# The last token group's routing: other PSUM banks, another place in the written order, later early gathers

## The chip, the cores and the metric

One core of one Trainium2 chip. The time is the device time of one execution in microseconds (us), the median of several runs; lower is better.

## The reference

Three layers, one after the other, over 3072 tokens (4 sequences of 768) of 384 features.

```python
# 1. delta-rule attention: per sequence and head (8 heads of 48), token after token
y[t] = q[t] @ state
state = state + beta[t] * outer(k[t], v[t] - k[t] @ state)      # k normalised
# 2. one MLP for all tokens: 384 -> 2048 -> 384
h = x @ w_in
x = maximum(0.01 * h, h) @ w_out
# 3. eight experts, each token goes to at most one: 384 -> 1024 -> 384
do = (x @ w_skip) > 0                       # the others are copied to the output
e = argmax(x @ w_gate); gate = softmax(x @ w_gate)[e]
out = x + gate * (maximum(x @ w1[e], 0) @ w2[e])    # where do, else x
```

Below, "the first layer" is layer 2 (`moe1` in the code) and "the experts" are layer 3 (`moe2`).

## The kernel before

Every fp32 operand is split into a high and a low fp16 half, and a product is three matmuls (high x high, high x low, low x high).

**Groups.** Tokens are worked on in 12 groups of 256 (two tiles of 128). A group goes through the attention stages and then the first layer in eight steps of two slices of 128 of the 2048 hidden features. Step `s` is an up (`m_up`, 18 matmuls into a bank `ph`; then ACT, DVE, ACT and POOL make the halves `ghh` and `gll`) and a down (`m_down`, 12 matmuls into two banks `o`). `w_gate` and `w_skip` are folded into ten more columns of `w_out` (columns HD to XW, 384 to 393), so that a down also yields the ten scores of a token. A normal group takes all 394 columns at once and is then routed (`m_fin`, `route`).

**The last group** (`moe1_last`, i = 11) is done apart. Its ups use the pool `h2`. Its downs go twice over the same operands: first only the ten score columns (key "r"), then the 384 others. Both sums are in the pool `ops`, which has two banks: the wide downs get them when ACT has copied the scores to `sc` (L987). Then a thread `last_route` is put at the head of the list of threads.

**Routing** (`route`). DVE and ACT find the best expert as a one-hot row `oh` (L740). After a yield PE counts, with a triangle of ones, the tokens of each expert before this one (`pr`, L746 to L750), DVE turns that into a place `pi` in the expert's part of a list in DRAM (L756 to L761), and POOL scatters the token numbers there, one indirect DMA for each tile of 128 (`lst`, L763). Each of the two waits for the one before. `pr` is in the pool `hps` (one bank, which the first layer's ups used) but for the last group, where it is in `tps` (one bank).

**Tables.** `early` runs after group 10 is routed: it counts (`counts`, a matmul and a copy, L1018 to L1020), finds up to three blocks of 256 tokens of one expert that are full already, and writes their table. `tables`, after the last group's route, counts again and writes the tables of the other blocks. The weights of a block are loaded when its table is there.

**Blocks.** The experts run as 15 blocks: 3 early, 6 big (two tiles of 128), 3 small (128 tokens) and 3 tiny (64). `Block.tokens` reads the block's stretch of the list on SP (`ix`, L1162), gathers its rows from `x2s` with an indirect DMA on POOL for each tile (`xg`, L1165), waits, then transposes them on PE into `pt` in the pool `tps` (L1173), from which ACT and DVE make the halves `xh` and `xl`. `up` and `down` (L1188, L1206 to L1208) follow, then the output is scattered (L1219). Weights come in eight loads of 384 KB for a block (L1138, L1141) through five buffers `ws`, and ACT and DVE split them (L441, L442). `early` calls `tokens` of blocks 0 and 1, the thread `tokens` of those from 2 on, once the tables are written. The rows of the last group are stored to `x2s` by SP (`store`, L714) after its wide downs.

**What sets the order.** Work is written as threads (Python generators). `emit` takes the first thread in its list whose time has come. A `yield a, w` adds `a` to a counter (about microseconds of PE work) and holds the thread for `w` more. What is written earlier has the higher priority, and `high_priority(n)` raises what is in it by n instructions. Dependences follow the written order: an instruction that reads a DRAM tile waits for the earlier written writes to it, and a write for the earlier written reads. A planner then fixes the order of each engine's instructions by priority and by its own estimate of when operands are there; on the chip every engine works off that order. Loads and stores are issued by SP, and its queue is in order too.

Of the kernel before, what the change touches and what calls it, by code (L numbers as in the profile page):

```python
# [8 lines left out]
F32 = mybir.dt.float32  # L9
# [10 lines left out]
HD = H * D  # L20
# [3 lines left out]
NS1 = NF1 // 2  # L24
# [5 lines left out]
XW = HD + 10  # L30
# [463 lines left out]
def tile_kernel(ctx, tc, kq, ktok, vtok, bet, w_in, w_out, w_skip, w_gate, w1, w2, out):  # L494
# [223 lines left out]
    def route(i, sc, t0s, then=lambda: None):  # L718

        L = sc[:, :, 1:9]  # L720
        sk = sc[:, :, 9:10]
        t = lambda nm, shape, dt=F32: rp.tile(shape, dt, tag=nm, name=nm)
        bc = lambda x: x.to_broadcast([128, 2, NE])
        mx, e1, sm, eq, m8, do, oh, ps = (t("mx", [128, 2, 1]), t("e1", [128, 2, NE]), t("sm", [128, 2, 1]),
                                          t("eq", [128, 2, NE]), t("m8", [128, 2, 1]), t("do", [128, 2, 1]),
                                          t("oh", [128, 2, NE], F16), t("ps", [128, 2, NE]))
        nc.vector.tensor_reduce(out=mx, in_=L, axis=AX.X, op=ALU.max)
        nc.vector.tensor_tensor(out=e1, in0=L, in1=bc(mx), op=ALU.subtract)
        nc.scalar.activation(out=e1, in_=e1, func=AF.Exp)
        nc.vector.tensor_reduce(out=sm, in_=e1, axis=AX.X, op=ALU.add)  # L730
        nc.vector.tensor_scalar_add(out=sm, in0=sm, scalar1=1e-9)
        nc.vector.reciprocal(out=sm, in_=sm)
        nc.vector.tensor_scalar_mul(out=sc[:, :, 0:1], in0=sm, scalar1=2.0 ** -13)
        then()
        nc.vector.tensor_tensor(out=eq, in0=L, in1=bc(mx), op=ALU.is_equal)
        nc.vector.tensor_tensor(out=eq, in0=eq, in1=wdesc.unsqueeze(1).to_broadcast([128, 2, NE]), op=ALU.mult)
        nc.vector.tensor_reduce(out=m8, in_=eq, axis=AX.X, op=ALU.max)
        nc.vector.tensor_tensor(out=eq, in0=eq, in1=bc(m8), op=ALU.is_equal)
        nc.vector.tensor_scalar(out=do, in0=sk, scalar1=0.0, scalar2=None, op0=ALU.is_gt)
        nc.vector.tensor_tensor(out=oh, in0=eq, in1=bc(do), op=ALU.mult)  # L740
        yield 0, T["rt"]
        pr = (hps if i < n - 1 else tps).tile([128, 512], F32, tag="h" if i < n - 1 else "t", name="pr")
        acc = acc_state[0]
        prv = pr[:, 0:2 * NE].rearrange("p (j e) -> p j e", j=2)
        for j in range(2):
            nc.tensor.matmul(prv[:, j], lhsT=tri16, rhs=oh[:, j], start=True, stop=(i == 0 and j == 0))  # L746
            if j == 1:
                nc.tensor.matmul(prv[:, j], lhsT=ones16, rhs=oh[:, 0], start=False, stop=(i == 0))
            if i:
                nc.tensor.matmul(prv[:, j], lhsT=ones16, rhs=acc, start=False, stop=True)  # L750
        nacc = t("acc", [128, NE], F16)
        nc.vector.tensor_tensor(out=nacc, in0=oh[:, 0], in1=oh[:, 1], op=ALU.add)
        if i:
            nc.vector.tensor_tensor(out=nacc, in0=nacc, in1=acc, op=ALU.add)
        acc_state[0] = nacc
        nc.vector.tensor_tensor(out=ps, in0=prv, in1=ebase.unsqueeze(1).to_broadcast([128, 2, NE]), op=ALU.add)  # L756
        nc.vector.tensor_tensor(out=ps, in0=ps, in1=oh, op=ALU.mult)
        pf = t("pf", [128, 2, 1])
        nc.vector.tensor_reduce(out=pf, in_=ps, axis=AX.X, op=ALU.add)
        pi = t("pi", [128, 2, 1], I32)  # L760
        nc.vector.tensor_scalar_add(out=pi, in0=pf, scalar1=float(BIG))  # L761
        for j in range(2):
            nc.gpsimd.indirect_dma_start(out=lst[:, :], out_offset=bass.IndirectOffsetOnAxis(ap=pi[:, j, 0:1], axis=0),  # L763
                                         in_=ids[:, t0s[j] // 128:t0s[j] // 128 + 1], in_offset=None,
                                         bounds_check=NL - 1, oob_is_err=False)
# [21 lines left out]
            nc.gpsimd.tensor_tensor(out=gl, in0=g, in1=gh, op=ALU.subtract)  # L787
        ms[i, s] = (gh, gl)

    def m_down(i, s, cols, key):  # L790
        if s == 0:
            ms[key] = [ops.tile([128, XW], F32, tag="o", name="o") for j in range(2)]
        gh, gl = ms[i, s]
        for j in range(2):
            f = 2 * s + j
            for t in range(2):
                ts = slice(t * 128, (t + 1) * 128)
                o = ms[key][t][:, cols]
                nc.tensor.matmul(o, lhsT=gh[:, j, ts], rhs=wo[0][:, f, cols], start=(f == 0), stop=False)  # L799
                nc.tensor.matmul(o, lhsT=gh[:, j, ts], rhs=wo[1][:, f, cols], start=False, stop=False)  # L800
                nc.tensor.matmul(o, lhsT=gl[:, j, ts], rhs=wo[0][:, f, cols], start=False, stop=(f == NF1 - 1))  # L801
            yield (cols.stop - cols.start) / 394, 0
# [175 lines left out]

    def moe1_last():
        i = n - 1  # L980
        for s in range(NS1):
            yield from m_up(i, s, m8 if s < NS1 - LOOK - 2 else m3, h2)
        for s in range(NS1):
            yield from m_down(i, s, slice(HD, XW), "r")
        sc = rp.tile([128, 2, 10], F32, tag="sc", name="sc")
        for t in range(2):
            nc.scalar.activation(out=sc[:, t], in_=ms["r"][t][:, HD:XW], func=AF.Copy, scale=2.0 ** -14)  # L987
        threads.insert(0, Thread(last_route(i, sc), lambda: "early" in state))
        for s in range(NS1):
            yield from m_down(i, s, slice(0, HD), i)  # L990
        xs = m_out(i, i, slice(0, HD))
        nc.vector.tensor_copy(out=xs[:, :, HD:HD + 1], in_=sc[:, :, 0:1])
        store(xs, first(i))
        lctx.close()
        et.append(pool(ctx, "eu", 1, **late))
# [18 lines left out]
    col = lambda x, n: x.unsqueeze(2).to_broadcast([1, x.shape[1], n])  # L1014

    def counts(nm):
        pr = tps.tile([128, 512], F32, tag="t", name="cnt")
        nc.tensor.matmul(pr[:, 0:NE], lhsT=ones16, rhs=acc_state[0], start=True, stop=True)  # L1018
        cnt = t1("cnt" + nm, [NE])
        nc.vector.tensor_copy(out=cnt, in_=pr[0:1, 0:NE])  # L1020
        return cnt
# [40 lines left out]
    def early():  # L1062

        nb = above(counts("e"), 255.5, "e")
        cb = upto(nb, "e")
        a, b, zero, taken = (t1(x, [NE]) for x in ("mine", "mina", "zero", "taken"))
        nc.vector.memset(zero, 0.0)
        table(nb, cb, zero, NEB, "early")
        tt(a, cb, nb, ALU.subtract)
        nc.vector.tensor_scalar_min(out=a, in0=a, scalar1=float(NEB))  # L1070
        nc.vector.tensor_scalar_min(out=b, in0=cb, scalar1=float(NEB))
        tt(taken, b, a, ALU.subtract)
        state["taken"] = taken
        yield 0, 4
        for b in blocks[:NEB - 1]:
            yield from b.tokens()

# [32 lines left out]
    class Block:  # L1110
# [47 lines left out]
        def tokens(self):  # L1158
            nt, R, N = self.nt, self.rows, self.nt * self.rows
            sl = bass.ds(self.entry(1, NL - N), N)  # L1160
            ix = self.idx = e3.tile([128, nt], I32, tag=f"ix{nt}", name="ix")[0:R]
            nc.sync.dma_start(out=ix, in_=lst[sl, :].rearrange("(p j) o -> p (j o)", j=nt))  # L1162
            xg = self.xg = self.tile([128, nt, HD + 1], F32, "xg")[0:R]
            for j in range(nt):
                nc.gpsimd.indirect_dma_start(out=xg[:, j], out_offset=None, in_=x2s[:, :],  # L1165
                                             in_offset=bass.IndirectOffsetOnAxis(ap=ix[:, j:j + 1], axis=0),
                                             bounds_check=NT, oob_is_err=False)
            yield 0, 7
            self.x = xh, xl = [self.tile([128, KD, nt * 128], F16, f"x{x}")[:, :, 0:N] for x in "hl"]
            for j in range(nt):  # L1170
                pt = tps.tile([128, KD, 128], F32, tag="t", name="pt")[:, :, 0:R]
                for d in range(KD):
                    nc.tensor.transpose(pt[:, d], xg[:, j, d * 128:(d + 1) * 128], ident[0:R, 0:R])  # L1173
                ts = slice(j * R, (j + 1) * R)
                nc.scalar.activation(out=xh[:, :, ts], in_=pt, func=AF.Copy, scale=32.0)
                nc.vector.scalar_tensor_tensor(out=xl[:, :, ts], in0=pt, scalar=32.0, in1=xh[:, :, ts], op0=ALU.mult, op1=ALU.subtract)
                yield .4, 1
            self.tok = True
# [106 lines left out]
    te = Thread(early())  # L1285
    tl1 = Thread(moe1_last())
    threads = [te] + threads + [tl1]
    emit(threads, lambda: tl1.done)
    mctx.close()
    threads += [Thread(tokens(), lambda: "nbi" in state), Thread(moe2())]  # L1290
    emit(threads)
# [60 lines left out]
```

## Time and profile before

| | |
|---|---|
| three runs | 1123.02, 1125.24 and 1130.80 us; median 1125.24 us |
| the profiled execution | 1127.62 us, its span 1125.8 us, mean granted TensorE clock 0.906 |
| busy in that span | PE 881.0 us (78%), DVE 724.2 (64%), ACT 658.6 (58%), POOL 500.9 (44%) |
| DMA queue of SP and ACT loads | q1: 123.24 MB, 42.4% of 16 engines' span |

All times in the rows are counted from the start of the span. PE is TensorE's matmul row, PEld its weight loads, SPq the instructions by which SP issues DMAs. A matmul's duration overlaps the next one's, so that the spacing of starts, not the duration, tells what it costs. What stands behind "<-" in a wait is the one that ended it.

### The profile page before, as it was taken

What the parts mean: (1) busy time and instruction counts of PE and PEld (TensorE: products, weight loads), DVE (VectorE), ACT (ScalarE), POOL (GpSimd) and SP (SyncE); (2) the same over time, 40 slices, a digit from 0 to 9 for tenths busy, and PEclk for the clock granted to TensorE, in tenths of its full rate; (3) what the DMA queues carried; (4) which work ended last, traced back from release to release, by engine and by line L of the source; (5) the groups of instructions that cost most, each with busy time, mean ns of one, the idle gap of its engine ahead of it and who ended that gap; (6) DMA issues with size and microseconds to landing.
All of it is one profiled execution on the core that took longest, in us unless ns stands there. A gap on an engine that the chain in (4) does not pass through costs nothing. (4 is left out here: it accounts for less than half of the span.)

```text
span 1125.8 us, 26420 instructions
## 1 busy us (share of the span) xinstructions
PE 881.0 (78%) x10212; PEld 679.8 (60%) x10212; DVE 724.2 (64%) x1599; ACT 658.6 (58%) x1494; POOL 500.9 (44%) x517
## 2 busy tenths in 40 slices
PE   2155887589798868876789797999985948998995
PEld 1144775466676656655667575777763636776763
DVE  5988986586665878655657374434236737887761
ACT  4477686567767767665767465553334516665640
POOL 3556565663365465746464353352243113342111
PEclk9998886589799988978899898999997969999998
DMA  7843876642434456625333322120007638988740
GB/s 207 217 123 101 236 209 177 131 125 37 140 84 95 135 95 196 96 68 121 79 82 64 32 55 39 44 30 29 29 29 178 215 100 251 293 292 279 245 145 17
DMA packets 200865, 144.03 MB, mean 128 GB/s; under 512 B 114318, under 2 KB 183140, under 8 KB 200730
## 3 DMA queue, kind: packets, MB, share of 16 engines
q1 hardware_dynamic: 188416, 123.24, 42.4%
q10 hardware_dynamic: 8570, 10.76, 3.4%
q0 software_dynamic: 3744, 8.27, 2.2%
q8 instruction: 82, 1.34, 0.6%
q14 instruction: 53, 0.43, 0.2%
HBM read 111.91 MB, written 30.92 MB: 127 GB/s over the span
## 5 line engine op out<-in xcount | busy, mean ns | idle before, releaser
L787 POOL TENSOR_TENSOR gll<-gg,ghh 128x512 f16<-128x512 f32 x96 | 114.4, 1194 | 133.7 <-ACT ghh L785 125.3
L783 DVE SCALAR_TENSOR_TENSOR gg<-gg 128x512 f32<-128x512 f32 x96 | 83.2, 868 | 97.6 <-ACT gg L782 97.2
L799 PE MATMUL o<-woh,ghh 128*128 128x394 f16 (+2 forms) x416 | 133.7, 329 | 12.6 <-ACT ghh L785 6.2
L777 PEld LDWEIGHTS <-wih 128*128 128x128 f16 x1152 | 115.7, 103 | 34.2 <-issue 11.9
L801 PE MATMUL o<-woh,gll 128*128 128x394 f16 (+2 forms) x416 | 125.1, 326 | 13.1 <-POOL gll L787 13.0
L800 PE MATMUL o<-wol,ghh 128*128 128x394 f16 (+2 forms) x416 | 133.9, 328 | 0.0
L263 POOL TENSOR_TENSOR gl<-g,gh 128x512 f16<-128x512 f32 x88 | 107.5, 1226 | 45.3 <-ACT gh L262 42.0
L254 ACT ACTIVATE g<-g,d 128x128 f32<-128x128 f32 x384 | 111.4, 384 | 26.7 <-PE g L251 22.4
L777 PE MATMUL ph<-xh,wih 128*128 128x256 f16 x576 | 103.2, 288 | 8.2 <-ACT gg L782 4.1
L255 POOL TENSOR_SCALAR_AFFINE_SELECT g<-g 128x512 f32<-128x512 f32 x96 | 69.3, 722 | 82.7 <-ACT g L254 75.4
L777 PE MATMUL ph<-xh,wil 128*128 128x256 f16 x576 | 102.7, 283 | 0.0
L777 PE MATMUL ph<-xl,wih 128*128 128x256 f16 x576 | 101.4, 286 | 1.1 <-DVE xl L707 1.1
L785 ACT CAST ghh<-gg 128x512 f16<-128x512 f32 x96 | 60.3, 628 | 71.4 <-DVE gg L783 70.5
L782 ACT COPY gg<-ph 128x512 f32<-128x512 f32 x96 | 57.0, 595 | 50.0 <-PE ph L777 46.4
L262 ACT CAST gh<-g 128x512 f16<-128x512 f32 x88 | 55.4, 633 | 35.7 <-POOL g L255 35.3
L442 DVE SCALAR_TENSOR_TENSOR w1l<-ws,w1h 128x768 f16<-128x768 f32 x60 | 57.4, 965 | 26.2 <-ACT w1h L441 24.6
L284 DVE TENSOR_TENSOR tmp<-bt,z 128x15 f32<-128x15 f16 (+4 forms) x180 | 58.7, 326 | 22.2 <-DMA bt<-ai 18.8
L1219 POOL DMA_INDIRECT out_dram<-y,ix x24 | 27.3, 1139 | 102.2 <-DVE y L1217 84.7
L441 ACT ACTIVATE w1h<-ws 128x768 f16<-128x768 f32 x60 | 49.7, 840 | 36.8 <-DMA ws<-in_moe_w_dram 30.4
L1188 PEld LDWEIGHTS <-w1h 128*128 128x128 f16 x720 | 59.1, 100 | 17.3 <-issue 5.5
L1165 POOL DMA_INDIRECT xg<-x2s,ix x24 | 35.6, 1484 | 68.6 <-DMA ix<-lst 48.6
L1206 PE MATMUL o<-w2h,gh 128*128 128x384 f16 (+1 forms) x192 | 63.4, 330 | 1.3 <-ACT gh L1192 1.3
(271 smaller groups left out, 2619.7 us busy)
## 6 DMA issues: line engine op xcount, KB each, us to landing
ws<-in_moe_w_dram SPq DMA_DIRECT2D x120, 384.0 KB
kt<-in_ktok_dram SPq DMA_DIRECT2D x24, 384.0 KB
x<-in_kq_dram SPq DMA_DIRECT2D x22, 384.0 KB
sc<-hl SPq DMA_DIRECT2D x22, 384.0 KB
raw<-in_moe_w_out_dram ACTq DMA_DIRECT2D x16, 384.0 KB
ai<-gh SPq DMA_DIRECT2D x24, 256.0 KB
x2s<-xs SPq DMA_DIRECT2D x24, 192.5 KB
vs<-in_vtok_dram SPq DMA_DIRECT2D x24, 192.0 KB
```

Source lines behind the costliest of these rows:

```text
L254: nc.scalar.activation(out=g32[:, j], in_=g[:, j], func=AF.Copy, scale=k["dd"][:, x, h:h + 1])
L255: nc.gpsimd.affine_select(out=g32, in_=g32, pattern=[[0, 4], [1, C]], compare_op=ALU.is_gt, fill=0.0, base=0, channel_multiplier=-1)
L263: nc.gpsimd.tensor_tensor(out=gl[:, hs], in0=g32, in1=gh[:, hs], op=ALU.subtract)
L777: nc.tensor.matmul(ph[:, j], lhsT=wt[:, d, fs], rhs=xx[:, d], start=(n == 0), stop=(n == 3 * KD - 1))
L783: nc.vector.scalar_tensor_tensor(out=g, in0=g, scalar=0.01, in1=g, op0=ALU.mult, op1=ALU.max)
L785: nc.scalar.copy(out=gh, in_=g)
L787: nc.gpsimd.tensor_tensor(out=gl, in0=g, in1=gh, op=ALU.subtract)
L799: nc.tensor.matmul(o, lhsT=gh[:, j, ts], rhs=wo[0][:, f, cols], start=(f == 0), stop=False)
L800: nc.tensor.matmul(o, lhsT=gh[:, j, ts], rhs=wo[1][:, f, cols], start=False, stop=False)
L801: nc.tensor.matmul(o, lhsT=gl[:, j, ts], rhs=wo[0][:, f, cols], start=False, stop=(f == NF1 - 1))
L1188: nc.tensor.matmul(ph[:, j], lhsT=wt[:, d, fs], rhs=xx[:, d], start=(n == 0), stop=(n == 3 * KD - 1))
L1206: nc.tensor.matmul(o, lhsT=gh[:, j, ts], rhs=wh[:, f], start=(f == 0), stop=False)
```

## The change

Six edits. The last group's `pr` and both `counts` move from `tps` to `hps`. `m_down` takes the pool of its sums, and the last group's scores go to `ops2`, a pool of two banks that the experts use later. The scores of step s - 2 are written after the up of step s, the wide down of step 0 ahead of the last two scores. `last_route` is written with a priority raised by 150. In `early` the list reads and gathers of blocks 0 and 1 are written 12 units behind their table instead of 4. In `tokens` the transposes of every block are written 11 units behind its gathers instead of 7. The first loop of `emit` goes on until the tables are written as well.

```diff
@@ -739,7 +739,7 @@
         nc.vector.tensor_scalar(out=do, in0=sk, scalar1=0.0, scalar2=None, op0=ALU.is_gt)
         nc.vector.tensor_tensor(out=oh, in0=eq, in1=bc(do), op=ALU.mult)
         yield 0, T["rt"]
-        pr = (hps if i < n - 1 else tps).tile([128, 512], F32, tag="h" if i < n - 1 else "t", name="pr")
+        pr = hps.tile([128, 512], F32, tag="h", name="pr")
         acc = acc_state[0]
         prv = pr[:, 0:2 * NE].rearrange("p (j e) -> p j e", j=2)
         for j in range(2):
@@ -787,9 +787,9 @@
             nc.gpsimd.tensor_tensor(out=gl, in0=g, in1=gh, op=ALU.subtract)
         ms[i, s] = (gh, gl)
 
-    def m_down(i, s, cols, key):
+    def m_down(i, s, cols, key, pl=ops):
         if s == 0:
-            ms[key] = [ops.tile([128, XW], F32, tag="o", name="o") for j in range(2)]
+            ms[key] = [pl.tile([128, XW], F32, tag="o", name="o") for j in range(2)]
         gh, gl = ms[i, s]
         for j in range(2):
             f = 2 * s + j
@@ -978,15 +978,19 @@
 
     def moe1_last():
         i = n - 1
+        scores = lambda s: m_down(i, s, slice(HD, XW), "r", ops2)
         for s in range(NS1):
             yield from m_up(i, s, m8 if s < NS1 - LOOK - 2 else m3, h2)
-        for s in range(NS1):
-            yield from m_down(i, s, slice(HD, XW), "r")
+            if s >= LOOK:
+                yield from scores(s - LOOK)
+        yield from m_down(i, 0, slice(0, HD), i)
+        for s in range(NS1 - LOOK, NS1):
+            yield from scores(s)
         sc = rp.tile([128, 2, 10], F32, tag="sc", name="sc")
         for t in range(2):
             nc.scalar.activation(out=sc[:, t], in_=ms["r"][t][:, HD:XW], func=AF.Copy, scale=2.0 ** -14)
-        threads.insert(0, Thread(last_route(i, sc), lambda: "early" in state))
-        for s in range(NS1):
+        threads.insert(0, Thread(high(last_route(i, sc), 150), lambda: "early" in state))
+        for s in range(1, NS1):
             yield from m_down(i, s, slice(0, HD), i)
         xs = m_out(i, i, slice(0, HD))
         nc.vector.tensor_copy(out=xs[:, :, HD:HD + 1], in_=sc[:, :, 0:1])
@@ -1014,7 +1018,7 @@
     col = lambda x, n: x.unsqueeze(2).to_broadcast([1, x.shape[1], n])
 
     def counts(nm):
-        pr = tps.tile([128, 512], F32, tag="t", name="cnt")
+        pr = hps.tile([128, 512], F32, tag="h", name="cnt")
         nc.tensor.matmul(pr[:, 0:NE], lhsT=ones16, rhs=acc_state[0], start=True, stop=True)
         cnt = t1("cnt" + nm, [NE])
         nc.vector.tensor_copy(out=cnt, in_=pr[0:1, 0:NE])
@@ -1071,7 +1075,7 @@
         nc.vector.tensor_scalar_min(out=b, in0=cb, scalar1=float(NEB))
         tt(taken, b, a, ALU.subtract)
         state["taken"] = taken
-        yield 0, 4
+        yield 0, 12
         for b in blocks[:NEB - 1]:
             yield from b.tokens()
 
@@ -1165,7 +1169,7 @@
                 nc.gpsimd.indirect_dma_start(out=xg[:, j], out_offset=None, in_=x2s[:, :],
                                              in_offset=bass.IndirectOffsetOnAxis(ap=ix[:, j:j + 1], axis=0),
                                              bounds_check=NT, oob_is_err=False)
-            yield 0, 7
+            yield 0, 11
             self.x = xh, xl = [self.tile([128, KD, nt * 128], F16, f"x{x}")[:, :, 0:N] for x in "hl"]
             for j in range(nt):
                 pt = tps.tile([128, KD, 128], F32, tag="t", name="pt")[:, :, 0:R]
@@ -1285,7 +1289,7 @@
     te = Thread(early())
     tl1 = Thread(moe1_last())
     threads = [te] + threads + [tl1]
-    emit(threads, lambda: tl1.done)
+    emit(threads, lambda: tl1.done and "nbi" in state)
     mctx.close()
     threads += [Thread(tokens(), lambda: "nbi" in state), Thread(moe2())]
     emit(threads)
```

## Rows read from the trace of the kernel before

**Rows 1.** Busy time by stretches: length, each engine's busy us (instructions), TensorE clock, DMA share, GB/s.
```profile
849.00:862.40 13.40, 1.79 (x45) 1.38 (x42) 4.75 (x10) 4.52 (x9) 4.68 (x4) 0.67 0.86 160
862.40:881.00 18.60, 18.60 (x102) 10.78 (x102) 14.85 (x31) 12.02 (x18) 5.28 (x4) 0.87 0.90 287
...
905.40:920.40 15.00, 0.33 (x4) 0.05 (x2) 1.28 (x8) 0.00 (x0) 3.08 (x3) 0.60 0.52 157
920.40:926.00 5.60, 5.60 (x24) 3.59 (x25) 2.62 (x15) 2.55 (x4) 1.00 (x1) 0.56 0.20 75
926.00:1112.60 186.60, 174.56 (x1530) 126.93 (x1527) 133.95 (x207) 103.97 (x166) 52.18 (x39) 0.98 0.72 229
...
890.00:912.00 22.00, 15.71 (x127) 11.74 (x125) 14.01 (x50) 4.78 (x8) 2.02 (x2) 0.92 0.15 38
```

**Rows 2.** Waits of PE, 849 to 863: who waited for whom, total us, times, longest.
```profile
PE o L799 <- ACT sc L987: 4.3, 1, 4.3
```

**Rows 3.** Timeline of PE, 881 to 921: start us, us, instruction, idle before and releaser.
```profile
884.86 0.52 PE L1173 MATMUL pt<-ident,xg 128*128 128x128 f32 x3 [2.10 <-DMA xg<-x2s,ix]
...
894.41 0.17 PE L746 MATMUL pr<-oh,tri 128*128 128x8 f16 x1
...
904.35 0.33 PE L1207 MATMUL o<-w2l,gh 128*128 128x384 f16 x1
904.51 0.33 PE L1208 MATMUL o<-w2h,gl 128*128 128x384 f16 x1
...
905.00 0.49 PE L1188 MATMUL ph<-xl,w1h 128*128 128x256 f16 x3
905.33 0.38 PE L1188 MATMUL ph<-xh,w1l 128*128 128x256 f16 x2
920.38 0.90 PE L1173 MATMUL pt<-ident,xg 128*128 128x128 f32 x3 [14.68 <-DMA xg<-x2s,ix]
```

**Rows 4.** Lines 1188 and 1206, 881 to 905.5: count, shortest, median, longest ns, starts.
```profile
L1188 PE MATMUL ph<-xl,w1h x39: 270/273/273, 881.7 to 905.2; 128*128 128x256 f16 x39
...
L1206 PE MATMUL o<-w2h,gh x16: 326/326/336, 888.3 to 904.2; 128*128 128x384 f16 x16
```

**Rows 5.** Timeline of ACT around the last group's scores.
```profile
861.44 0.84 ACT L441 ACTIVATE w1h<-ws 128x768 f16<-128x768 f32 x1 [4.55 <-DMA ws<-in_moe_w_dram]
862.19 0.23 ACT L987 ACTIVATE sc<-o 128x10 f32<-128x10 f32 x2
```

**Rows 6.** Timeline of DVE: routing of group 10 and of the last group.
```profile
838.73 0.17 DVE L727 TENSOR_REDUCE mx<-xs 128x2 f32<-128x16 f32 x1 [1.20 <-ACT xs L811]
...
840.60 0.17 DVE L740 TENSOR_TENSOR oh<-eq,do 128x16 f16<-128x16 f32 x1
...
867.86 0.15 DVE L740 TENSOR_TENSOR oh<-eq,do 128x16 f16<-128x16 f32 x1
...
896.12 0.17 DVE L761 TENSOR_SCALAR pi<-pf 128x2 int32<-128x2 f32 x1
```

**Rows 7.** Timeline of POOL: the last group's list scatters and block 2's gather.
```profile
896.57 1.02 POOL L763 DMA_INDIRECT lst<-ids_i,pi  x1 [15.12 <-DVE pi L761]
903.71 1.00 POOL L763 DMA_INDIRECT lst<-ids_i,pi  x1 [6.12 <-DMA lst<-ids_i,pi]
913.59 1.05 POOL L1165 DMA_INDIRECT xg<-x2s,ix  x1 [8.88 <-DMA ix<-lst]
```

**Rows 8.** Timeline of SP's DMA queue.
```profile
910.01 0.34 SPq L1162 DMA_DIRECT2D ix<-lst  x1
```

**Rows 9.** Waits of SP's DMA queue, 881 to 921.
```profile
SPq L1162 <- DMA lst<-ids_i,pi: 19.2, 1, 19.2
SPq L714 <- DMA xg<-x2s,ix: 3.3, 1, 3.3
```

**Rows 10.** Line 763, the 24 list scatters of the whole run.
```profile
DMA to landing us min/median/max: 6.8/7.2/8.8
```

**Rows 11.** Waits of PE, 926 to 1114.
```profile
PE pt L1173 <- DMA xg<-x2s,ix: 8.7, 6, 2.7
```

## The prediction

> **What bounds the kernel now.** I read the 40 slices of the page first, then busy time by stretches around the hand-over from the first layer to the experts, then the waits, last each engine's timeline there. Three things are to be seen.
>
> PE is the busiest engine, but not evenly. From 849 to 862.4 us it works 1.79 of 13.40 us, from 905.4 to 920.4 us 0.33 of 15.00, while in the long stretch from 926 to 1112.6 it is at work for 174.56 of 186.60 us [rows 1]. After 926 nearly every microsecond is PE work, so what is saved before it should reach the end, as long as nothing else takes over. What follows 1112.6 (the last scatters and the ending) isn't touched.
>
> The first hole has several waits in it, the largest for `sc`: 4.3 us [rows 2], since the same two banks hold the narrow score sums and the wide down sums. The second is one wait of 14.68 us: PE stands at the transposes of block 2 until its rows have been gathered [rows 3]. It isn't out of work there. From 881 to 905.4 us 116 up matmuls (39, 39 and 38 of three kinds; one kind is shown) and 48 down matmuls (three kinds of 16) ran [rows 4]; a block of 256 tokens has 72 and 48. So 28 up and 48 down matmuls of block 1 stand behind the transposes in PE's fixed order. By the spacing of starts an up matmul costs 0.33/3 = 0.109 us and a down matmul 0.16 [rows 3]: 28 x 0.109 + 48 x 0.1625 = 10.9 us left of block 1 at 920.4. A whole block is 72 x 0.109 + 48 x 0.1625 + six transposes at 0.11 = 16.3 us.
>
> Why is block 2 late? The last group's choice of experts is ready on DVE at 868.0 (867.86 + 0.17) [rows 6], but its counting matmuls `pr` run on PE at 894.41 [rows 3]: their bank is that of the transposes, handed out after block 1's, which ran at 884.86 and later. From there: `pi` at 896.29 [rows 6], two scatters into the list at 896.57 and 903.71 [rows 7], the list read by SP at 910.01 [rows 8] after a wait of 19.2 us on the scatters [rows 9], the gather at 913.59 [rows 7], the transposes at 920.38 [rows 3].
>
> **The change, part by part.**
>
> *Counts in the first layer's bank, route ahead of other work.* `pr` no longer queues behind the transposes. Lower bound for `pi`: `sc` ends at 862.42 (862.19 + 0.23) [rows 5]; group 10 took 2.04 us from its first DVE step to `oh` (838.73 to 840.77) [rows 6]; from `pr` to `pi` took 1.9 (894.41 to 896.29) [rows 3, 6]: 866.3. Upper bound: 5.6 us to `oh`, as now between weight splits: 870.0. The route is placed ahead of the splits, so I take 3 us, `pi` at 867.3. The 4.55 us for which ACT waited ahead of `sc`, on a weight load [rows 5], I leave in: nothing in the change moves that load. The early count now waits for group 10's counts to be read from the same bank, at most the 1.9 us from `pr` to `pi`; ups of the last group cover it on PE, and uncovered it would delay the first weights by as much.
>
> *The scatters.* Issue 0.3 us after `pi` (896.29 to 896.57), 867.6. The pair took 13.4 us (896.57 to 910.01) [rows 7, 8] in a stretch in which the DMA engines were 0.15 busy; between 862.4 and 881 they were 0.90 busy [rows 1]. All 24 scatters landed in 6.8 to 8.8 us [rows 10], so two cost 13.4 to 17.6; I take the middle, 15.5. List complete at 883.1. DMA: Bandwidth & Descriptors in the Trainium skill (Queues, rings and completion order) says that a completion lands only after every earlier write of that DMA engine, across its queues; by that rule scatters put among weight loads pay the upper end, and the gain below is 2.1 us smaller.
>
> *Early gathers later.* This is not a delay of a few microseconds only. I added up the waits that the hand-written order gives its threads. Before, block 1's list read is written at 13.8 units of PE work after the last group starts, the last scatters at 26.8. After, both fall at 27.9, and the route's thread stands first in the list. So block 1 now reads the list behind the last scatters and must wait for both, as block 2 did. From the list's read to the transposes took 10.4 us (910.01 to 920.38) [rows 3, 8]; about 2 us more for the second tile, whose gather stands behind the first's 1.05 us [rows 7], and its copies. Block 1 can run at 883.1 + 12.4 = 895.5.
>
> PE will again stand at transposes before it is out of work. Now 10.9 us of PE work lie between `pr` and the transposes of block 2 (894.41 to 905.33, PE not idle) [rows 3]; the same distance behind a `pr` that sits in the downs puts block 1's transposes 1 to 6 us into block 0. The written order has them 6.1 units behind its start (38.9 against 32.8). I take 5. Then at 895.5 there are left 11.3 us of block 0 and 16.3 of block 1, 27.6, where the kernel before has 10.9 left at 920.4: the same point comes at 895.5 + 16.7 = 912.2, a gain of 8.2 us. Both restart at a low clock (the granted clock was 0.56 from 920.4 to 926 [rows 1], some 2.5 us), which cancels.
>
> *Scores in their own banks, two steps behind.* The same matmuls, moved. The downs can fill the first hole: by itself 0 to 11.6 us (13.40 - 1.79). I count none of it: the downs finish sooner, and PE then waits for block 1's rows all the same. If the chain of scatters were not the end, this would be the gain.
>
> *Transposes 11 instead of 7 behind their gathers.* This holds for every later block. From 926 on PE lost 8.7 us in six waits for gathered rows, none over 2.7 [rows 11]; four units later could take away all of it. A later place can cost too, where a block waits for its transposes; I bound that by four, the shift itself. Between -4 and +8.7 I take the middle, 2.4, as neither end has a row of its own.
>
> Holding the loop until the tables are written costs nothing: by the same addition they are written at 31.8, before the last down at 32.8. If not, PE's work on block 0 would be written later, not run later.
>
> Sum: 8.2 + 2.4 = 10.6 us. The profiled execution took 1127.62 us (its span 1125.8 and 1.8 around it): 1117.0. It was 2.4 us above the median of 1125.24, so against the median **1115 us**. Bounds: the list 3.1 us earlier (866.3 + 0.3 + 13.4 = 880.0) or 4.8 later (870.0 + 0.3 + 17.6 = 887.9), block 1's transposes from 1 us into block 0 (4 us worse) on, the last part 6.4 either way; not all together: 1104 to 1125 for this case.
>
> **The rivals.**
>
> *The stall is swallowed (faster).* If block 1's transposes stand at the end of block 0, or its read ahead of the scatters, PE has block 0 to do meanwhile: 16.3 - 5 = 11.3 us more, a gain of 19.5 + 2.4 = 22: 1103, from 1096 to 1106 with the ends of the last part. For it: PE waited only 2.1 us at block 1's transposes so far [rows 3]. Against it: the distance from `pr` that the order shows for a chain through two scatters.
>
> *The store stands behind block 1's gather (slower).* The last group's rows go to `x2s` by an SP store that waits until earlier gathers have read; it already waited 3.3 us [rows 9]. Now block 1's gather is the late one, and block 2's gather follows the store. Gather landed at about 894.5, some 6 us for the two stores (no row; between 0 and a scatter's largest 8.8 [rows 10]), a gather's issue to transposes 6.8 (913.59 to 920.38) [rows 3, 7], 2 for the second tile: 909.3. If block 2's transposes stand only 5 us behind block 1's, PE waits from 903 on, with 22.6 us left at 909.3, 11.7 more than the 10.9: 921.0, and a second slow start, 2.5, 923.5: 3.1 us behind the kernel before, 7.1 with the last part at -4, 11.9 with the late list. 1128 to 1138, and 1137 at the full price. It decides from the point where block 2's rows come later than PE reaches their transposes, about 10 us of work behind block 1's. Against it: so far 20 us of work lay between the two (884.86 to 905.33) [rows 3].
>
> *It doesn't take.* If `pr` stays behind other work on PE until 894, block 0 alone runs meanwhile and block 1 is ready at 910.0 + 12.4 = 922.4 with 16.3 left where 10.9 were at 920.4: 7.4 us slower, 1133; somewhat early, 1125.
>
> **How the numbers follow.** Forecast 0.50, stall swallowed 0.22, store 0.17, doesn't take 0.11. About 1% (11 us) is what a measurement of this kernel tells from no change: faster means under 1114, slower over 1136.5. Faster: 0.22 and some 0.42 of the forecast, 0.43. Slower: half of the store case, a fifth of the last one and 0.04 for an order that I don't foresee, 0.15. Same: 0.42. The range, 1099 to 1136, leaves out the best third of the swallowed case, about half of the store case and the unforeseen: some 0.19.
>
> **What would show it.** `pr` near 866 instead of 894; the list's scatters done by 880 to 888; the SP queue waiting on them before block 1's read, and the long PE wait at block 1's transposes, near 895, instead of block 2's at 920. No wait of PE on `sc`. If the hole before 862 fills and the end still moves little, the chain of scatters was the bound. I am wrong if block 1's rows are there before the scatters, if PE's long wait is at block 2 again, or if waits on gathered rows after 926 grow.

## The result, and the profile after

The changed kernel takes 1116.2 us (median of 20 runs, 1108.2 to 1122.8), the kernel before beside it 1126.5 (20 runs): a ratio of 0.990 [0.988, 0.993], or 10.3 us less by the medians. Ratios here and below leave out slow runs (of the kernel before up to 10 of 35) and medians don't, so that the two can differ by up to 4 us. The profiled execution took 1114.44 us, its span 1112.7. Lines from 987 on stand four further down than before.

First the stretches around the hand-over (view and columns as in [rows 1]):

```profile
846.80:868.50 21.70, 18.06 (x128) 10.30 (x125) 11.43 (x33) 10.11 (x16) 4.42 (x4) 0.92 0.81 205
868.50:881.00 12.50, 0.45 (x6) 0.21 (x6) 8.88 (x22) 6.82 (x10) 3.87 (x3) 0.59 0.95 307
881.00:900.00 19.00, 11.45 (x72) 8.04 (x72) 13.39 (x41) 7.89 (x12) 3.15 (x3) 0.82 0.46 115
900.00:912.70 12.70, 11.15 (x68) 7.57 (x69) 7.14 (x30) 4.72 (x7) 1.99 (x2) 0.87 0.75 240
```

The hole ahead of the last down sums is nearly gone: PE is idle for 3.64 of 21.70 us, and the sums end at 867.4 instead of 881. But the 12.5 us that follow are a new hole, 0.45 us of work. The timeline of PE (columns as in [rows 3]) says what stands there:

```profile
868.51 0.18 PE L746 MATMUL pr<-oh,tri 128*128 128x8 f16 x1 [1.09 <-DVE oh L740]
...
873.67 0.17 PE L1022 MATMUL cnt<-acc,ones 128*128 128x8 f16 x1 [4.88 <-DVE ps L756]
881.08 0.90 PE L1177 MATMUL pt<-ident,xg 128*128 128x128 f32 x3 [7.24 <-DMA xg<-x2s,ix]
...
900.65 0.55 PE L1177 MATMUL pt<-ident,xg 128*128 128x128 f32 x3 [3.44 <-DMA xg<-x2s,ix]
...
912.40 0.52 PE L1177 MATMUL pt<-ident,xg 128*128 128x128 f32 x3 [0.90 <-DVE o L1015]
```

`pr` runs at 868.51 instead of 894.41 [rows 3], and the 14.68 us wait for block 2's rows has gone. The longest wait for rows is now that of block 0, 7.24 us at 881.08; block 1's transposes wait 3.44 us. The route on DVE:

```profile
862.55 0.16 DVE L727 TENSOR_REDUCE mx<-sc 128x2 f32<-128x16 f32 x1
...
868.28 0.17 DVE L740 TENSOR_TENSOR oh<-eq,do 128x16 f16<-128x16 f32 x1
...
868.92 0.96 DVE L442 SCALAR_TENSOR_TENSOR w1l<-ws,w1h 128x768 f16<-128x768 f32 x1 [0.38 <-ACT w1h L441]
...
875.02 0.15 DVE L761 TENSOR_SCALAR pi<-pf 128x2 int32<-128x2 f32 x1
```

It still alternates with splits of 0.95 us each: 5.7 us from its first step to `oh`, 6.5 from `pr` to `pi`. POOL, and SP's queue:

```profile
873.76 1.04 POOL L1169 DMA_INDIRECT xg<-x2s,ix  x1 [20.06 <-DMA ws<-in_moe_w_dram]
875.11 1.80 POOL L1169 DMA_INDIRECT xg<-x2s,ix  x1 [0.31 <-issue]
877.22 1.02 POOL L763 DMA_INDIRECT lst<-ids_i,pi  x1 [0.30 <-DVE nbl L1032]
888.00 1.00 POOL L763 DMA_INDIRECT lst<-ids_i,pi  x1 [9.76 <-DMA lst<-ids_i,pi]
897.28 1.14 POOL L1169 DMA_INDIRECT xg<-x2s,ix  x1 [8.28 <-DMA ix<-lst]
```

```profile
868.96 0.35 SPq L1166 DMA_DIRECT2D ix<-lst  x1
...
877.10 10.14 SPq L1145 DMA_DIRECT2D ws<-in_moe_w_dram  x4
894.80 0.86 SPq L1166 DMA_DIRECT2D ix<-lst  x2
901.91 0.81 SPq L714 DMA_DIRECT2D x2s<-xs  x2
```

Block 0's list read is issued at 868.96 and its gather at 873.76, behind weight loads; the scatters stand behind that gather on POOL, and block 1's read behind the scatters, at 894.80. So block 1's read did move behind the scatters. In the long stretch after 926 PE waits less for rows and a little more for `gl` (before: 8.7 in six [rows 11], and 2.5 in four for `gl`):

```profile
PE ph L1192 <- DVE gl L1198: 3.9, 5, 1.6
PE pt L1177 <- DMA xg<-x2s,ix: 2.2, 2, 1.5
```

To see where the time came from I cut PE's idle time at 930 us in both kernels, from 845 us to PE's last work. Before, then after:

```profile
845.00:930.00 85.00, 56.03 (x446) 39.12 (x445) 49.37 (x141) 33.03 (x53) 18.50 (x16) 0.82 0.58 167
930.00:1112.60 182.60, 170.56 (x1498) 123.85 (x1496) 130.23 (x194) 102.19 (x164) 52.18 (x39) 0.98 0.73 232
```

```profile
845.00:930.00 85.00, 58.75 (x425) 40.07 (x423) 54.95 (x159) 40.35 (x61) 18.79 (x16) 0.86 0.72 212
930.00:1099.20 169.20, 162.97 (x1465) 118.24 (x1463) 120.40 (x176) 94.63 (x153) 48.69 (x37) 1.00 0.71 228
```

PE's work ends at 1099.2 instead of 1112.6, 13.4 us sooner. Idle time (length less PE's busy time) fell from 29.0 to 26.2 us up to 930 and from 12.0 to 6.2 behind it; of what is left of the 13.4, 3.4 us are less idle time ahead of 845 (2.3 of them ahead of 780, where the change moves nothing on PE) and 1.4 less time at work. So far the time agrees with the forecast, and the places do not.

### The profile page after: what moved, and what is told of

Its sections match the earlier page's. It is cut to its first block, busy times and chain, and to the rows that moved or that the text cites. A ratio compares the mean times of both kernels' runs of the same rounds, so it can differ in the third digit from the quotient of the medians.

```text
span 1112.7 us, 26421 instructions
## 1 busy us (share of the span) xinstructions
PE 879.6 (79%) x10212; PEld 676.2 (61%) x10212; DVE 720.9 (65%) x1599; ACT 658.6 (59%) x1494; POOL 500.9 (45%) x517
## 5 line engine op out<-in xcount | busy, mean ns | idle before, releaser
L777 PEld LDWEIGHTS <-wih 128*128 128x128 f16 x1152 | 116.4, 104 | 34.7 <-issue 11.7
L441 ACT ACTIVATE w1h<-ws 128x768 f16<-128x768 f32 x60 | 50.4, 841 | 43.7 <-DMA ws<-in_moe_w_dram 35.1
L284 DVE TENSOR_TENSOR tmp<-bt,z 128x15 f32<-128x15 f16 (+4 forms) x180 | 60.6, 337 | 20.5 <-DMA bt<-ai 17.1
L777 PEld LDWEIGHTS <-wil 128*128 128x128 f16 x576 | 58.6, 103 | 9.5
```

The source lines that it names most:

```text
L284: nc.vector.tensor_tensor(out=tmp[:, 0:t, 0:w], in0=bt[:, 0:t, t:t + 1].to_broadcast([128, t, w]), in1=z[:, t:t + 1, t:16].to_broadcast([1 ...
L777: nc.tensor.matmul(ph[:, j], lhsT=wt[:, d, fs], rhs=xx[:, d], start=(n == 0), stop=(n == 3 * KD - 1))
```

## The experiments

Ratios stand against the kernel before, run beside each; 1% is 11.2 us. The last two columns are PE's idle time of one profile each, cut as above. Ahead of 780 us none of the edits moves anything on PE, and yet its idle time there ranges from 180.6 to 191.5 us over these profiles, so that a few us in one column are no finding.

| kernel | median us (runs) | ratio [95%] | idle to 930 | behind 930 |
|---|---|---|---|---|
| before | 1126.5 (20) | 1 | 29.0 | 12.0 |
| changed | 1116.2 (20) | 0.990 [0.988, 0.993] | 26.2 | 6.2 |
| 11 alone | 1116.8 (12) | 0.992 [0.988, 0.996] | 19.2 | 12.1 |
| 11, first three blocks | 1114.8 (12) | 0.995 [0.991, 0.998] | 19.9 | 11.6 |
| 11, later blocks | 1122.4 (12) | 1.001 [0.997, 1.004] | 26.6 | 9.8 |
| bank alone | 1117.4 (12) | 0.994 [0.990, 0.997] | 18.5 | 10.0 |
| bank and 11 | 1114.9 (12) | 0.991 [0.987, 0.995] | 24.7 | 7.0 |
| scores and 11 | 1119.9 (12) | 0.999 [0.995, 1.002] | 25.1 | 8.5 |
| changed, 7 for 11 | 1131.3 (12) | 1.005 [1.001, 1.008] | 31.3 | 9.3 |
| changed, old scores | 1117.1 (12) | 0.992 [0.988, 0.996] | 25.1 | 6.2 |
| changed, both early reads at 4 | 1118.8 (12) | 0.994 [0.990, 0.998] | 26.5 | 7.3 |
| changed, block 0's read at 4 | 1115.2 (6) | 0.989 [0.984, 0.995] | 20.7 | 8.0 |
| the same, old scores | 1117.2 (12) | 0.994 [0.991, 0.997] | 24.7 | 4.9 |
| changed, splits held | 1121.5 (12) | 0.997 [0.994, 1.000] | 26.8 | 8.1 |

The sum of the two columns goes roughly with the ratio: 28.5 to 33.8 us up to 0.995, 33.6 to 41.0 from 0.997 on. Neither column does so alone.

**The 11 out of the changed kernel, and alone in the kernel before.**

```
             for j in range(nt):
             ...
-            yield 0, 11      # in the changed kernel; the second run has 11 for 7 in the kernel before
+            yield 0, 7
```

> The changed kernel with transposes 7 instead of 11 units behind their gathers. Theory: the later place is what took PE's waits for gathered rows after 926 us from 8.7 to 2.2 us; they come back to 6 to 9 us and the time rises 3 to 6 us, ratio to the kernel before 0.993 to 0.996. Rival: the late waits fell because the blocks started in another order of stalls, not by the 11: they stay under 4 us and the ratio stays at 0.990.

> The kernel before with transposes 11 instead of 7 units behind their gathers, alone. Theory: waits of PE for gathered rows after 926 us fall from 8.7 us to under 4, the 14.7 us wait for block 2 stays; ratio 0.994 to 0.998. Rival: block 2's transposes also move back by four units of work, so the long wait shrinks by 4 as well: ratio 0.990 to 0.994.

Without the 11 the rest of the change is 5.3 us slower than the kernel before (0.0047 x 1127.3); the 11 alone gives 8.8 us (0.0078 x 1127.3), nearly all that the change gives. Neither theory for the run with 7 had it slower than the kernel before. With the 11 alone, on PE:

```profile
882.00 0.17 PE L746 MATMUL pr<-oh,tri 128*128 128x8 f16 x1
...
909.04 0.87 PE L1173 MATMUL pt<-ident,xg 128*128 128x128 f32 x3 [4.07 <-DMA xg<-x2s,ix]
```

Block 1's transposes are written later, so `pr`, in the transposes' own bank, comes ahead of them: 31.2 us behind the early table's last step on DVE instead of 44.3 (in these two profiles that step is at 850.80 and 850.09), and the wait for block 2's rows falls from 14.68 us to 4.07. The changed kernel with 7 shows another order on SP's queue and on POOL (its profiled execution, 1123.1 us, is the fastest of its 12, 8.2 below their median, so that these rows show the order and not its price):

```profile
874.56 9.05 SPq L1145 DMA_DIRECT2D ws<-in_moe_w_dram  x4
883.79 1.16 SPq L1166 DMA_DIRECT2D ix<-lst  x1
```

```profile
887.67 1.72 POOL L763 DMA_INDIRECT lst<-ids_i,pi  x1 [13.56 <-DVE nbi L1108]
```

Here block 1's read is written ahead of the scatters, so they must wait for it, and it stands behind four weight loads that take 9.05 us to issue. `pi` is there at 872.22, the first scatter goes at 887.67. (The row names DVE as the releaser; in the program that scatter also waits for the read's queue, and the one of the changed kernel doesn't.) In the changed kernel the 11 is what takes the read out of the scatters' way. `pr` ahead of the transposes is not enough by itself: here it runs at 865.22, and nothing is gained.

**The 11 by halves, in the kernel before.**

```
-            yield 0, 7
+            yield 0, 11 if self in blocks[:NEB] else 7      # and the reverse
```

> The kernel before, with the distance of 11 from a block's gathers to its transposes for the first three blocks alone, 7 for all later ones. With 11 for all blocks and nothing else of the change the median was 1116.8 us, 0.992 of the kernel before. Theory P (the gain lies at the hand-over: transposes written later let the last group's counting matmuls and the scatters behind them come first, and shorten the wait for block 2's rows): about 1118 us, ratio 0.990 to 0.995, block 2's wait for rows near 4 us instead of 14.7, waits after it as in the kernel before. Theory L (as the prediction had it, the gain is that of the later blocks' waits for rows, 2.4 us, up to 8.7): 1125 to 1127 us, ratio 0.998 to 1.000.

> The opposite half: the kernel before, with 7 for the first three blocks and 11 for all later ones. Theory P: 1125 to 1128 us, ratio 0.998 to 1.001; the wait for block 2's rows stays at 14 to 15 us, and the waits for rows after 926 us (8.7 us in six) shrink, but what they give back is lost again to other waits. Theory L: 1118 to 1121 us, ratio 0.992 to 0.995.

For the first three blocks: 5.7 us [1.8, 9.7]. For the later ones: -0.9 [-4.7, 2.9]. Their PE rows, first three, then later:

```profile
877.41 0.17 PE L746 MATMUL pr<-oh,tri 128*128 128x8 f16 x1
...
903.84 0.87 PE L1173 MATMUL pt<-ident,xg 128*128 128x128 f32 x3 [5.24 <-DMA xg<-x2s,ix]
```

```profile
895.88 0.17 PE L746 MATMUL pr<-oh,tri 128*128 128x8 f16 x1
...
919.87 0.90 PE L1173 MATMUL pt<-ident,xg 128*128 128x128 f32 x3 [12.69 <-DMA xg<-x2s,ix]
```

The gain is at the hand-over; of the later blocks none can be told. (By the medians the halves give 9.7 and 2.1 us.)

**The bank alone, and with the 11.**

```
-        pr = (hps if i < n - 1 else tps).tile([128, 512], F32, tag="h" if i < n - 1 else "t", name="pr")
+        pr = hps.tile([128, 512], F32, tag="h", name="pr")
...
-        pr = tps.tile([128, 512], F32, tag="t", name="cnt")
+        pr = hps.tile([128, 512], F32, tag="h", name="cnt")
...
-    emit(threads, lambda: tl1.done)
+    emit(threads, lambda: tl1.done and "nbi" in state)
```

> The kernel before with the bank part alone: the last group's counts in the first layer's bank, the loop held until the tables are written; transposes at 7, scores and early reads as before. Theory P (the gain of the 11 lies in the order of `pr`, and moving `pr` by its bank brings the same): `pr` 20 to 30 us behind the early table instead of 44, 1115 to 1119 us, ratio 0.989 to 0.994. Theory Q (`pr` sooner is worth nothing while the scatters stand behind the gathers of block 1 in POOL's order, or while the transposes stand only 7 behind): 1123 to 1127 us, ratio 0.997 to 1.001, the scatters no more than 5 us sooner than in the kernel before and a wait of 8 us or more for rows.

> The kernel before with 11 for all blocks, and the last group's counts in the first layer's bank with the tables written before the loop ends; scores and early reads as before. If the chain of counts, scatters and gather still sets the end once the 11 is there (theory A): counting matmuls 5 to 10 us sooner than with the 11 alone (there 31 us after the early table), the 4.1 us that block 2's rows are still waited for go, 1112 to 1114 us, ratio 0.987 to 0.989. If it does not (theory B, the experts' work on PE and the splits of their weights set the end by then): 1116 to 1119 us, ratio 0.990 to 0.993.

The bank alone gives 7.1 us [3.0, 11.0], with `pr` at 17.8 us behind the early table. Its first scatter still stands behind block 1's gather on POOL:

```profile
866.26 0.17 PE L746 MATMUL pr<-oh,tri 128*128 128x8 f16 x1
...
880.62 0.88 PE L1173 MATMUL pt<-ident,xg 128*128 128x128 f32 x3 [3.56 <-DMA xg<-x2s,ix]
```

```profile
875.48 1.00 POOL L1165 DMA_INDIRECT xg<-x2s,ix  x1 [0.30 <-issue]
876.78 1.02 POOL L763 DMA_INDIRECT lst<-ids_i,pi  x1 [0.30 <-issue]
```

No wait for rows is longer than those 3.56 us. Both edits together give 10.5 us [5.8, 15.2], not the 15.9 of their sum. Time does not tell the two theories for the pair apart. In its profile `pr` comes at 19.8 us and the first scatter only at 35.1, again with block 1's gather ahead of it: with the 11, block 1's read goes out at 878.20 behind more weight loads, where the bank alone has 868.60. Block 2's rows are late again:

```profile
910.51 0.88 PE L1173 MATMUL pt<-ident,xg 128*128 128x128 f32 x3 [11.76 <-DMA xg<-x2s,ix]
```

So the pair does not fall short because each edit removes the same wait of 14.68 us, which could go only once: with both edits most of that wait is back, and the time is no worse for it. Idle time behind 930 is 7.0 us here, where either edit alone has 10 to 12; why is open.

**The scores: added to the 11, and taken out of the changed kernel.**

```
+        scores = lambda s: m_down(i, s, slice(HD, XW), "r", ops2)
...
-        for s in range(NS1):
-            yield from m_down(i, s, slice(HD, XW), "r")
+            if s >= LOOK:
+                yield from scores(s - LOOK)
+        yield from m_down(i, 0, slice(0, HD), i)
+        for s in range(NS1 - LOOK, NS1):
+            yield from scores(s)
```

> The kernel before with 11 for all blocks, and the last group's scores in banks of their own, two steps behind; counts' bank and early reads as before. Theory A: the down sums end 10 to 13 us sooner, PE then waits that much longer for rows, 1116 to 1118 us, ratio 0.990 to 0.992, as with the 11 alone. Theory B (PE's work sets the end, so a hole of PE that is filled is a gain): 1107 to 1110 us, ratio 0.982 to 0.985.

> The changed kernel without the part on the scores: they share the banks of the wide down sums again and stand behind all up matmuls; counts' bank, later early reads and the 11 stay. Theory A (what is gained ahead of 868 is lost to the wait for block 0's rows, so the part on the scores is worth nothing or less): 1113 to 1118 us, ratio 0.988 to 0.992, the hole in front of `sc` back with about 8 us of idle PE and the hole behind it shorter by as much. Theory B (filling the hole is a gain): 1121 to 1125 us, ratio 0.996 to 1.000.

On top of the 11 they leave 1.6 us [-2.2, 5.3] of the 8.8, a smaller gain than either theory had; the two intervals just touch, so a cost is likely and not certain. What PE no longer waits for `sc` it waits for rows, 26.4 us in all where the 11 alone has 9.5:

```profile
PE pt L1177 <- DMA xg<-x2s,ix: 26.4, 6, 8.4
```

Out of the changed kernel the median is 0.9 us higher, which is nothing that can be told. The filled hole is worth nothing that shows.

**Earlier reads in the changed kernel.** The first run puts both early reads at 4, the second block 0's alone.

```
-        yield 0, 12
+        yield 0, 4
         for b in blocks[:NEB - 1]:
             yield from b.tokens()
+            yield 0, 11      # second run only
```

> The changed kernel with 4 instead of 12 for both early blocks: block 1's read is then written ahead of the last scatters and doesn't wait for them. Theory A: PE has blocks 0 and 1 to do while the two scatters run, so waits of PE for gathered rows up to 925 us fall from about 12 us to under 6, and the time falls 4 to 8 us below the changed kernel, ratio 0.983 to 0.987. Theory B: the same as when block 0 alone is read early, ratio 0.983 to 0.986 for both. A rival that speaks for the change as it is: SP's queue stands at the early read and weights come later; then slower than the changed kernel, ratio 0.992 to 1.000.

> The changed kernel with block 0's list read written 4 units behind the early table instead of 12 (SP then issues it behind 6 weight loads, not 14); block 1's read stays behind the last scatters. Theory A, the chain of scores, two scatters, list read and gather sets when blocks 1 and 2 run: block 0's transposes move from 881 to about 873 us, PE's hole after 868 shrinks, but PE then waits longer at block 1's transposes; the time stays within 3 us of the changed kernel, ratio to the kernel before 0.988 to 0.993. Theory B, block 0's late rows are the bound: the end moves with the hole, 5 to 8 us earlier, ratio 0.983 to 0.986.

> The changed kernel with the old place of the scores, block 0's list read at 4 instead of 12, and block 1's read kept behind the scatters. Of the runs so far the parts that gained are in it and the part on the scores, which cost 0.6% on top of the 11, is out. Theory A (the chain of counts, scatters and gather no longer sets the end; PE's and the splits' work does): 1113 to 1117 us, ratio 0.988 to 0.992, like the changed kernel. Theory C (each wait that is taken away still counts): scatters at 24 to 40 us behind the early table, block 1's rows without a long wait, 1107 to 1111 us, ratio 0.982 to 0.986.

With block 0's read early and block 1's behind the scatters the new hole ahead of 881 shrinks (PE waits 5.58 us for block 0's rows, at 875.92), and the time is that of the changed kernel (0.989 against 0.990; with six runs the interval leaves up to 6 us either way). So far as these runs can tell, the hole was slack: PE waits at block 1's and block 2's transposes instead (3.9 and 3.0 us, where the changed kernel has 3.44 and none for rows). With both reads early, block 1's stands ahead of the scatters again, as in the changed kernel with 7, and here the row names it:

```profile
888.32 1.70 POOL L763 DMA_INDIRECT lst<-ids_i,pi  x1 [16.63 <-DMA ix<-lst]
```

Block 2's rows are then late, 11.2 us at 916.24. The third run, the second with the old scores, has next to no wait for rows left:

```profile
PE ph L1189 <- ACT xh L1176: 7.9, 2, 4.7
PE o L801 <- POOL gll L787: 4.8, 3, 3.3
PE o L799 <- ACT sc L987: 4.8, 1, 4.8
PE o L1207 <- ACT gh L1193: 3.7, 3, 2.5
PE ph L1189 <- DVE gl L1195: 3.3, 6, 0.8
...
PE pt L1174 <- DMA xg<-x2s,ix: 0.4, 2, 0.3
```

It is no faster than the changed kernel with the old scores alone (0.994 against 0.992), which waits 14.1 us for rows up to 930. The waits for `gll` and `sc` are the first hole, back with the old scores; new against that kernel are most of the 7.9 us for `xh`, the high halves of the rows that ACT makes (0.6 there). So rows are no longer the limit there, and no version that I ran beats the changed kernel by more than the intervals allow.

**The splits held behind the route.** In the changed kernel, block 1's splits (and the loads that their thread issues) wait for `pi`.

```
+            if i == 1:
+                yield 0, 0, lambda: "pi" in state
...
-                b.split()
+                    with tc.issue_after(state["pi"].ins):      # block 1 alone
+                        b.split()
```

> The changed kernel, with the splits of block 1's weights held on DVE until the last group's `pi` is there, which is where the prediction had put the route. Theory R (the splits between the steps of the route are what made `pi` come at 875.2 instead of 867.3, but the scatters stand behind block 0's gathers on POOL, so that little is gained): `pi` some 2 us behind the counting matmuls instead of 6.5, the first scatter 0 to 2 us sooner, 1114 to 1118 us, ratio 0.988 to 0.993. Theory S (the chain from `pi` on sets the end): 4 to 5 us less than the changed kernel, 1110 to 1112 us, ratio 0.984 to 0.987. Block 1's splits come up to 5 us later; if PE is held up by them, 1118 to 1121 us.

DVE, PE and SP's queue:

```profile
869.93 0.17 DVE L761 TENSOR_SCALAR pi<-pf 128x2 int32<-128x2 f32 x1
```

```profile
900.94 0.87 PE L1179 MATMUL pt<-ident,xg 128*128 128x128 f32 x3 [12.83 <-DMA xg<-x2s,ix]
```

```profile
868.66 0.37 SPq L1147 DMA_DIRECT2D ws<-in_moe_w_dram  x1
...
874.88 0.84 SPq L716 DMA_DIRECT2D out_dram<-xs  x2
891.32 0.35 SPq L1168 DMA_DIRECT2D ix<-lst  x1
891.92 1.65 SPq L1147 DMA_DIRECT2D ws<-in_moe_w_dram  x3
```

`pi` comes 0.95 us behind `pr` (868.98) instead of 6.51: the splits were the delay. But POOL issues the first scatter at 877.99, no sooner than in the changed kernel, since block 0's gathers stand ahead of it; the list is complete at 891.32 instead of 894.80, and block 1 starts at 900.94 where the changed kernel has 900.65. The run lost some 8 us to the changed kernel by the ratios (0.997 against 0.990; the intervals don't meet), 5 by the medians. SP issued no weight load from 869.0 to 891.9 us, first because the loads were held with the splits, then while its read waited for the scatters, where the changed kernel issued ten; that this is what cost the time was not tried by itself.

## Why the prediction was right, and where it was not

The number, 1115, was right, and so was the root: `pr` stood behind the transposes, and either edit that puts it ahead gives 7 to 9 us by itself in the kernel before, and takes most of the wait for block 2's rows away. That this wait is what the microseconds are, as the prediction has it, is not shown: the pair has 11.76 us of it and gains as much, and in the changed kernel, where it is gone, other waits at the hand-over leave idle time up to 930 only 2.8 us shorter. The sum got to 10.6 us by terms that were not what each part does, so that the nearness to the measured 10.3 is in good part luck.

- *`pr` near 866.* Right within 2.5 us: 868.51. The bank alone brings it to 866.26 and gives 7.1 us, where the forecast had 8.2 for it together with the later reads.
- *"The route is placed ahead of the splits, so I take 3 us, `pi` at 867.3."* Wrong: 875.02, 5 us beyond even the upper bound. Four splits and a wait for weights on ACT still stand ahead of `sc`, and the route alternates with splits. Written without the raised priority, the planned order is the same but for one pair on DVE; that version was not run. Held splits brought `pi` to 869.93 and gained nothing, since the scatters stand behind block 0's gathers on POOL, a queue that the sum did not count.
- *Two scatters, 15.5 us, list at 883.1.* 17.6 (877.22 to 894.80), the upper bound; the list was complete 11.7 us later than forecast.
- *Block 1's read behind the scatters, PE's long wait at its transposes near 895.* The first half is right, but only by the 11: with 7 the read stands ahead of them. The wait is at block 0's, which the sum had at no delay at all: its read slipped from 861.27 to 868.96 behind more weight loads. That hole was slack so far as the runs that narrowed it can tell.
- *Scores, counted 0.* Right in size out of the changed kernel; on top of the 11 alone they probably cost. What PE wins ahead of 868 is lost by 881.
- *"Transposes 11 instead of 7 ... I take the middle, 2.4."* The term that was mis-sized, and misplaced. I priced it on the six late waits [rows 11]; those waits did shrink in the changed kernel, and with the 11 on the later blocks alone from 8.7 us to 4.1 behind 930, but that run gave -0.9 us [-4.7, 2.9]. On the first three blocks it gave 5.7 us [1.8, 9.7], because it changes the order in which `pr`, scatters and reads are written. I priced its length and not what it moves past.
- *The store behind block 1's gather (the slower rival).* Seen, and harmless in this profile: it was issued at 901.91 after waiting 5.5 us for the gather, and block 2's transposes at 912.40 did not wait for rows.
- *The stall is swallowed; it doesn't take.* Neither: idle time to 930 fell by 2.8 us only, but `pr` did move.

The two halves of the sum were taken to add, 8.2 + 2.4. By the runs bank and 11 give 7.1 and 8.8 us alone, and together 10.5. What stays open: why they don't add, why idle time behind 930 falls to 6 or 7 us with both edits and stays at 10 to 12 with either (one profile each), and which of scores and later reads it is that makes the changed kernel with 7 slower than the bank alone (0.994 against 1.005).

## What to carry to other kernels

Where a planner writes one order for all queues, a number in it is not a delay: list what each moved step now stands ahead of and behind, on PE, POOL and SP, before pricing it in microseconds. Don't add up two edits at the same place: run each alone and both together, and look whether the wait that each removes alone is still gone with both. A hole in the busiest engine that was filled was worth nothing here, as the next thing that the engine waits for came no sooner.

## What was not expected of the hardware

Two scatters in a row, each issued when the one before has landed, took the longer the more the DMA engines moved beside them. The stretches from the first's issue to the list's read, in the run with held splits, the changed kernel, and the one with block 0's early read and old scores (second last number: DMA share):

```profile
878.00:891.30 13.30, 7.77 (x42) 5.45 (x42) 3.37 (x16) 0.98 (x2) 2.01 (x2) 0.70 0.08 17
```

```profile
877.20:894.80 17.60, 9.04 (x56) 6.50 (x57) 11.35 (x32) 8.14 (x12) 2.02 (x2) 0.69 0.66 181
```

```profile
875.00:894.10 19.10, 14.93 (x99) 10.01 (x96) 10.87 (x25) 8.68 (x13) 2.41 (x2) 0.91 0.99 192
```

13.3 us at a share of 0.08, 17.6 at 0.66, 19.1 at 0.99. In the other eleven profiles the pair took 12.8 to 15.1 us at shares up to 0.28 and 14.4 to 17.1 at 0.51 to 0.85 (in two of these with gathers between the two scatters): a trend, with inversions. By the rule weighed in the prediction (the Trainium skill, DMA: Bandwidth & Descriptors, Queues, rings and completion order) a completion lands behind every earlier write of its DMA engine, whichever queue that came from; the traces agree with it, and don't show that it is the cause. In the run with held splits, which keeps weight loads out of the scatters' way, the list is complete 3.5 us sooner, and the kernel is slower all the same.
